# Block products of an MLP: partial sums kept in SBUF, or added to DRAM by DMA

## The chip, the cores and the metric

The kernel runs on one core of a Trainium2 chip. The metric is device time in microseconds (us), the median over runs of the whole kernel. One execution was profiled; its trace gives the start, the duration and the waits of the instructions of each engine: TensorE (PE; its weight loads are PEld), VectorE (DVE), ScalarE (ACT), GpSimd (POOL) and SyncE (SP), which issues DMAs.

## The reference

The input x has 2048 rows of 576 numbers. It is normalized by rows, goes through an MLP with 4608 hidden features and through a two-dimensional Fourier transform of which the real part is kept, and all three are summed:

```python
xn = _layernorm(x, axis=-1)
# A: a = xn @ dft_hid_re.T, b = xn @ dft_hid_im.T
#    y = dft_seq_re @ a - dft_seq_im @ b
# B: relu(xn @ w1) @ w2
return x + A(xn) + B(xn)
```

All arrays are float32.

## The kernel before

Every float32 operand of a matmul is split into a high and a low float16 part, and three products of parts stand for one product. The work has three stages.

The **MLP** runs first. The hidden features are cut into NB = 9 blocks b of 512, the rows into NG = 4 groups g of 512; a step is one (b, g), 36 in all. `mlp1_step` makes the first layer of a step in four parts i, each of 128 hidden features by 512 rows (L292, L317). `mlp1_out` takes them through the ReLU and the splits to SBUF (L332 to L343). `mlp2` makes the second layer. It is a Strassen-Winograd scheme: each operand is cut into 2 x 2 blocks, and the four blocks of the product C (row half `row`, column half `col`, each 256 rows by 288 columns, held as 128 partitions x 2 x 288) come out of seven products n = 0 to 6. `PRODUCTS` says which block of C a product belongs to, and `PLACE` says in which PSUM buffer it is summed:

```python
    PRODUCTS = [
        (A11, B11, True, 0, 0),
        (A12, B21, True, 0, 0),
        (S2, T2, False, 0, 1),
        (S1, T1, True, 1, 1),
        (S3, T3, False, 1, 1),
        (S4, B22, False, 0, 1),
        (A22, T4, False, 1, 0),
    ]
    PLACE = [0, 1, 0, 3, 0, 3, 0]
```

So the first buffer goes on collecting products 0, 2, 4 and 6, and after each product the sum so far is read out and counts towards one block of C: products 0 and 1 to block (0,0), 2 and 5 to (0,1), 3 and 4 to (1,1), 6 alone to (1,0). Two buffers of the pool `ps2` hold the three places in turn. Each read-out is one VectorE instruction (L363) that scales by `us[b]` and adds to the accumulator `accs[g]` in SBUF. `accs[g]` holds four tiles of 128 rows of x (loaded at L80, and the input of the normalization), so x itself is the start value of the sum. After the last block of a group, four DMAs on SP store the tiles to the DRAM tiles `spill` (L366).

Steps are interleaved: the first layer of a step stands between products of the step before (part i, then products 2i and 2i + 1). Beside them run pieces of `todo`, one at a time: loading, scaling and splitting the next block's weights. For these, the largest magnitude is taken (L99, L414), brought across the partitions by GpSimd (L105, for blocks 2 and up; for blocks 0 and 1 by PE, L142 and L150) and read by VectorE (L108; L152, L424). In block 0 the groups 1 to 3 are also normalized on the way (statistics L184 to L206, `normalize` L226 and L227, `remainder` on GpSimd L231 and L234, `transposes` L242 to L252). The matrices of the sequence transform, C, are read once for their magnitude (`first_c`, `sum_c`: tile f, L665 and L672).

The **hidden transform** (`dft1`, L760 to L792) follows, and its results R lie in the SBUF space of the released pools. The **sequence transform** (L857 to L883) multiplies R by the matrices C, again in seven products, onto tiles `o`, which `load_out` fills from `spill` (L853), and stores them.

The order on each engine is made by the tile framework's scheduler when the kernel is built; each engine then works through its own list in that order. `tc.issue_after(order["acc"])` puts some instructions behind the last L363 issued.

Of the kernel before, what the change touches and what calls it, by code (L numbers as in the profile page):

```python
# [1 line left out]

# [7 lines left out]
F32 = mybir.dt.float32  # L10
BF16 = mybir.dt.bfloat16
I32 = mybir.dt.int32
AF = mybir.ActivationFunctionType
ALU = mybir.AluOpType
# [3 lines left out]
P = 128  # L18
S = 2048
D = 576  # L20
DFF = 4608
NT = S // P
FB = 512
NB = DFF // FB
# [3 lines left out]
NG = S // G  # L28
TG = G // P
# [4 lines left out]
EH = D // 2  # L34
# [7 lines left out]
def kernel(  # L42
# [17 lines left out]
    nc = tc.nc  # L60
# [3 lines left out]
    dram = ctx.enter_context(tc.tile_pool(name="dram", bufs=1, space=bass.MemoryType.DRAM))  # L64
# [8 lines left out]

    accs = [accp.tile([P, TG, D], F32, name=f"acc{g}") for g in range(NG)]
    acc = [accs[t // TG][:, t % TG] for t in range(NT)]
    spill = [dram.tile([P, D], F32, name=f"spill{t}") for t in range(NT)]
    raws = {}

    def load_x(t):
# [92 lines left out]
    means, factors, shifts, order = {}, {}, {}, {}  # L172
# [115 lines left out]
    w1s, w2s, us, hs = {}, {}, {}, {}  # L288

    def mlp1_group(b, g, i, cols, ps, wk=WK, start=True, stop=True):  # L290
        for n, (kx, hl, k) in enumerate(wk):
            nc.tensor.matmul(  # L292
                ps[:, cols], w1s[b, i // 2][:, hl, i % 2 * KT + k], xT[g][:, kx, cols],
                start=(start and n == 0), stop=(stop and n == len(wk) - 1),
            )

    def new_ps1(b, g, i):
        return ps1.tile([P, G], F32, tag="ps1", name=f"p1_{b}_{g}_{i}")

    def mlp1(b, g, i):  # L300
        ps = new_ps1(b, g, i)
        mlp1_group(b, g, i, slice(0, G), ps)
        return ps
# [38 lines left out]
        order["s"] = nc.scalar.activation(hi, st[:, 1:], AF.Copy).ins  # L342
        order["lo"] = nc.vector.tensor_tensor(lo, st[:, 1:], hi, ALU.subtract).ins  # L343

    places = {}

    def mlp2(b, g, n):

        qa, qb, first, row, col = PRODUCTS[n]
        if first:  # L350
            places[n] = ps2.tile([P, 2, 512], F32, tag="ps2", name=f"p2_{b}_{g}_{n}")[:, :, :EH]
        ps = places[PLACE[n]]
        for c in range(2):
            for i in range(NQ):
                h, w = hs[b, g, i], w2s[b, i]
                for j, (x, y) in enumerate(((0, 0), (0, 1), (1, 0))):
                    nc.tensor.matmul(  # L357
                        ps[:, c], h[:, x, qa, c * P : (c + 1) * P], w[:, y, qb],
                        start=first and i == 0 and j == 0, stop=i == NQ - 1 and j == 2,
                        skip_group_check=not first,  # L360
                    )
        o = accs[g].rearrange("p (h c) (j e) -> p h j c e", h=2, j=2)[:, row, col]
        order["acc"] = nc.vector.scalar_tensor_tensor(o, ps, us[b], o, ALU.mult, ALU.add).ins  # L363
        if b == NB - 1 and n == 6:
            for t in range(g * TG, (g + 1) * TG):
                nc.sync.dma_start(spill[t], acc[t])  # L366

    sc, pw, mx = {}, {}, {}

# [140 lines left out]
    ps = [ps1.tile([P, G], F32, tag="ps1", name=f"p1_0_0_{i}") for i in range(NF)]  # L510
# [86 lines left out]
    T(10)  # L597
    T(11)
    early = [mlp1(0, 2, 0), mlp1(0, 2, 1)]
    for q in range(7):  # L600
        mlp2(0, 0, q)

# [47 lines left out]
    NP = NT // 2  # L650
# [28 lines left out]
    for n in range(2, len(steps)):  # L679
        b, g = steps[n]  # L680
# [15 lines left out]
        ps = []  # L696
        for i in range(NF):
            if n == 2:
                ps.append(early.pop(0) if early else mlp1(b, g, i))
            else:  # L700
                mlp1_step(b, g, i, ps)
            if i % 2:
                mlp1_out(b, g, i // 2, *ps[i - 1 : i + 1])
            if b == 0 and g + 1 < NG:
                t = (g + 1) * TG + i
                normalize(t)
                remainder(t, nc.gpsimd)
                transposes(t)
            if n == 2 and i == 2:
                todo += prepare_block(1)  # L710
            for _ in range(1 if b else 3):
                work()
            for q in range(2 * i, min(2 * i + 2, 7)):
                mlp2(pb, pg, q)
            for _ in range(1 if b else 3):
                work()
            if n > 3 and i % 2 and passes:
                passes.pop(0)()
    while todo:
        work()  # L720
    for q in range(7):
        mlp2(*steps[-1], q)
# [127 lines left out]
    def load_out(p):  # L850
        o = outs[p] = op.tile([P, 2, D], F32, tag="o", name=f"o{p}")
        for h in range(2):
            nc.sync.dma_start(o[:, h], spill[p + h * NP])  # L853

    AHEAD = 3
    load_out(0)
    for n, (p, kh) in enumerate(units):  # L857
        if kh == 0 and p + 1 < NP:
            load_out(p + 1)
        if n + 1 < len(units):  # L860
            load_c(n + 1)
        for i, (q, rq, first, row, col) in enumerate(PRODUCTS):
            m = n * 7 + i
            if m + AHEAD < 7 * len(units):
                operand(m + AHEAD)
            if first:
                places[i] = bank(f"p{n}_{i}")
            ps, w = places[PLACE[i]], csp[m]
            for k in range(HK):
                r = R[kh * HK + k]  # L870
                for j, (a, c) in enumerate(((0, 0), (0, 1), (1, 0))):
                    nc.tensor.matmul(  # L872
                        ps, w[:, a, k], r[:, c, rq],
                        start=first and k == 0 and j == 0, stop=k == HK - 1 and j == 2,
                        skip_group_check=not first,
                    )
            o = outs[p][:, row, col * EH : (col + 1) * EH]
            nc.vector.scalar_tensor_tensor(o, ps, us["c"][:, n : n + 1], o, ALU.mult, ALU.add)  # L878
            if kh and i in (2, 4, 5, 6):
                h, j = ((0, 0), (1, 1), (0, 1), (1, 0))[(2, 4, 5, 6).index(i)]  # L880
                rows = slice((p + h * NP) * P, (p + h * NP + 1) * P)
                e = slice(j * EH, (j + 1) * EH)
                nc.sync.dma_start(out[rows, e], outs[p][:, h, e])  # L883
# [54 lines left out]
```

## Time and profile before

| | us |
|---|---|
| median of 3 runs | 1285.52 (1283.52 to 1285.96) |
| the profiled execution | 1283.83 |
| its span, first to last instruction | 1282.0 |
| PE, DVE, ACT, POOL busy | 1264.8, 980.5, 539.0, 36.5 |
| a step of the MLP, from block 1 on | 22.16 |
| the sequence transform on PE | 329.3 |

Busy times are unions of the instructions' times; the instructions of a stage overlap between engines, so they do not add up to the span. An engine's idle time matters only where the chain of waits that ends last goes through it. A group's row gives the line, the engine, the operation, output <- input, the shapes, the count, then busy time, mean ns of one, idle time before them and what ended most of it.

### The profile page before, as it was taken

How to read it: one execution, taken by the hardware profiler on the slowest of the kernel's cores; microseconds unless marked ns; L12 is line 12 of the kernel's file. 1: busy time of each engine (PE TensorE's matmuls, PEld its weight loads, DVE VectorE, ACT ScalarE, POOL GpSimd, SP SyncE). 2: the span in 40 equal slices, each digit the busy share in tenths (PEclk: the TensorE clock that was granted, in tenths of full speed). 3: DMA queues.
4: the chain of work that ended last, by engine and by line, in shares of the span. 5: the costliest groups of instructions: out<-in, count | busy, mean ns of one | idle time of the engine just before them, and what ended most of it. 6: DMA issues, size and time to landing. Idle time of an engine off the chain costs nothing.

```text
span 1282.0 us, 21851 instructions
## 1 busy us (share of the span) xinstructions
PE 1264.8 (99%) x9164; PEld 859.2 (67%) x9164; DVE 980.5 (76%) x1671; ACT 539.0 (42%) x794; POOL 36.5 (3%) x60
## 2 busy tenths in 40 slices
PE   8799999999999999999999999999999999999998
PEld 7565665666565665666565665677777777777777
DVE  8978877786686687777867868568678788888875
ACT  5834443343443443434434434244443333333332
POOL 2310000000000000000000000000000000000000
PEclk8999999999999999999999999999999999999999
DMA  6102112221221222122222213330033435334320
GB/s 243 43 1 68 56 59 91 86 77 65 87 91 68 64 79 68 69 91 87 69 73 86 97 57 110 112 132 17 1 114 124 155 101 167 121 125 133 130 85 19
DMA packets 38002, 112.75 MB, mean 88 GB/s; under 512 B 3984, under 2 KB 10640, under 8 KB 37904
## 3 DMA queue, kind: packets, MB, share of 16 engines
q1 hardware_dynamic: 37904, 111.36, 25.9%
q8 instruction: 71, 1.16, 0.4%
q14 instruction: 27, 0.22, 0.0%
HBM read 101.91 MB, written 9.44 MB: 87 GB/s over the span
## 4 chain that ended last, share of the span: by engine, by line
PE 91%; DVE 5%; ACT 1%; DMA 1%; issue 1%; SPq 0%; POOL 0%; POOLq 0%; ACTq 0%; DVEq 0%
PE p L292 29%; PE p L357 27%; PE p L872 26%; PE pd L760 7%; PE p L317 1%; DVE acc L363 1%; DVE w2s L167 1%; DVE xn L226 0%; DVE w1s L167 0%; DMA acc<-in_x_dram 0%; DVE st L184 0%; DMA c<-in_cre_dram 0%; DVE h L336 0%; PE pd L770 0%; ACT xn L227 0%
## 5 line engine op out<-in xcount | busy, mean ns | idle before, releaser
L292 PE MATMUL p<-xT,w1s 128*128 128x512 f16 (+1 forms) x2136 | 434.7, 355 | 1.3 <-ACT xT L249 1.1
L357 PE MATMUL p<-w2s,h 128*128 128x288 f16 x3024 | 394.6, 286 | 2.0 <-ACT xT L252 1.0
L357 PEld LDWEIGHTS <-h 128*128 128x128 f16 x3024 | 295.3, 98 | 103.0 <-issue 2.8
L872 PE MATMUL p<-R,cs 128*128 128x288 f16 x2688 | 329.4, 286 | 0.0
L292 PEld LDWEIGHTS <-w1s 128*128 128x128 f16 x2136 | 193.5, 98 | 201.9 <-issue 18.4
L872 PEld LDWEIGHTS <-cs 128*128 128x128 f16 x2688 | 263.0, 98 | 66.3
L363 DVE SCALAR_TENSOR_TENSOR acc<-p,c_ub,acc 128x576 f32<-128x576 f32 x252 | 204.8, 813 | 39.0 <-PE p L357 38.5
L166 ACT ACTIVATE cs<-c,sc_c 128x1024 f16<-128x1024 f32 x112 | 128.5, 1148 | 200.2 <-PE p L872 147.5
L167 DVE SCALAR_TENSOR_TENSOR cs<-c,sc_c,cs 128x1024 f16<-128x1024 f32 x112 | 143.7, 1283 | 50.3 <-ACT cs L166 50.1
L336 DVE SCALAR_TENSOR_TENSOR h<-p,h 128x256 f16<-128x256 f32 (+1 forms) x144 | 79.8, 555 | 94.8 <-ACT h L335 94.5
L342 ACT ACTIVATE h<-s 128x1024 f16<-128x1024 f32 x72 | 76.1, 1057 | 160.5 <-DVE s L340 160.4
L335 ACT ACTIVATE h<-p 128x256 f16<-128x256 f32 (+1 forms) x144 | 69.9, 486 | 147.2 <-PE p L292 141.4
L343 DVE TENSOR_TENSOR h<-s,h 128x1024 f16<-128x1024 f32 x72 | 88.1, 1224 | 31.2 <-ACT h L342 30.2
L760 PE MATMUL pd<-dsp,xT 128*128 128x288 f16 x832 | 104.0, 286 | 0.2
L760 PEld LDWEIGHTS <-xT 128*128 128x128 f16 x832 | 80.7, 98 | 22.6 <-issue 2.5
L878 DVE SCALAR_TENSOR_TENSOR o<-p,us_c,o 128x288 f32<-128x288 f32 x112 | 57.6, 514 | 20.3 <-PE p L872 20.3
L672 ACT ACTIVATE f<-f 128x1024 f32<-128x1024 f32 x64 | 66.6, 1041 | 3.7 <-DMA f<-in_cre_dram 3.7
L332 ACT ACTIVATE s<-p 128x256 f32<-128x256 f32 x72 | 27.4, 380 | 74.0 <-PE p L317 54.5
L166 ACT ACTIVATE w2s<-raw_w,c_sw 128x576 f16<-128x576 f32 (+1 forms) x54 | 44.2, 851 | 25.9 <-DVE raw_w L445 15.4
L167 DVE SCALAR_TENSOR_TENSOR w2s<-raw_w,c_sw,w2s 128x576 f16<-128x576 f32 (+1 forms) x54 | 48.5, 916 | 7.6 <-ACT w2s L166 7.6
L167 DVE SCALAR_TENSOR_TENSOR w1s<-raw_w,c_sw,w1s 128x640 f16<-128x640 f32 x36 | 30.8, 892 | 9.8 <-ACT w1s L166 9.8
L166 ACT ACTIVATE w1s<-raw_w,c_sw 128x640 f16<-128x640 f32 x36 | 27.9, 817 | 24.0 <-DVE c_sw L109 23.6
(106 smaller groups left out, 672.5 us busy)
## 6 DMA issues: line engine op xcount, KB each, us to landing
f<-in_cre_dram SPq DMA_DIRECT2D x32, 512.0 KB, 3.5
f<-in_cim_dram SPq DMA_DIRECT2D x32, 512.0 KB, 3.5
c<-in_cre_dram SPq DMA_DIRECT2D x32, 512.0 KB, 4.0
c<-in_cim_dram SPq DMA_DIRECT2D x32, 512.0 KB, 4.6
raw_w<-in_w_dram SPq DMA_DIRECT2D x17, 640.0 KB, 4.0
raw_w<-in_w_dram SPq DMA_DIRECT2D x18, 576.0 KB, 3.8
acc<-in_x_dram SPq DMA_DIRECT2D x16, 288.0 KB, 7.4
spill<-acc SPq DMA_DIRECT2D x16, 288.0 KB, 2.5
```

The source lines that it names most:

```text
L166: nc.scalar.activation(hi, src, AF.Copy, scale=s)
L167: nc.vector.scalar_tensor_tensor(lo, src, s, hi, ALU.mult, ALU.subtract)
L292: nc.tensor.matmul(ps[:, cols], w1s[b, i // 2][:, hl, i % 2 * KT + k], xT[g][:, kx, cols], start=(start and n == 0), stop=(stop and n == l ...
L335: nc.scalar.activation(hi, src, AF.Relu)
L336: stt(lo, src, 0.0, hi, ALU.max, ALU.subtract)
L342: order["s"] = nc.scalar.activation(hi, st[:, 1:], AF.Copy).ins
L343: order["lo"] = nc.vector.tensor_tensor(lo, st[:, 1:], hi, ALU.subtract).ins
L357: nc.tensor.matmul(ps[:, c], h[:, x, qa, c * P : (c + 1) * P], w[:, y, qb], start=first and i == 0 and j == 0, stop=i == NQ - 1 and j == 2 ...
L363: order["acc"] = nc.vector.scalar_tensor_tensor(o, ps, us[b], o, ALU.mult, ALU.add).ins
L672: nc.scalar.activation(f, f, AF.Abs, scale=2.0**-10, accum_out=sums_c[:, n, q : q + 1])
L760: nc.tensor.matmul(ps[j], xT[g][:, kx, c * P : (c + 1) * P], dsp[j][:, hl, k], start=(t % 2 == 0 and n == 0), stop=(t % 2 == 1 and n == le ...
L872: nc.tensor.matmul(ps, w[:, a, k], r[:, c, rq], start=first and k == 0 and j == 0, stop=k == HK - 1 and j == 2, skip_group_check=not first,)
```

## The change

The accumulator over blocks moves from SBUF to DRAM. For each group and each block of C there is now one DRAM tile of `spill`, and x is copied into it from DRAM by 16 DMAs on SP before the first product is read out (`spill_x`). In each step, the first product of a block of C (n = 0, 2, 3, 6) is scaled by ScalarE into one of four slots of `accs[0]`, which are taken in turn; the second (n = 1, 5, 4) is scaled and added there by VectorE; then one DMA on GpSimd's queue adds the slot to the DRAM tile. Product 6 has no second. The stores behind the last block go away, and `load_out` reads half rows from two tiles.

```diff
-    spill = [dram.tile([P, D], F32, name=f"spill{t}") for t in range(NT)]
+    spill = {
+        (g, row, col): dram.tile([P, TG // 2, EH], F32, name=f"spill{g}_{row}{col}")
+        for g in range(NG) for row in range(2) for col in range(2)
+    }
...
-    places = {}
+    places, sums = {}, {}
+    turns = itertools.count()
+
+    def spill_x(g):
+        for row in range(2):
+            for col in range(2):
+                src = x[(g * TG + row * 2) * P : (g * TG + row * 2 + 2) * P, col * EH : (col + 1) * EH]
+                nc.sync.dma_start(spill[g, row, col], src.rearrange("(c p) e -> p c e", p=P))
...
-        o = accs[g].rearrange("p (h c) (j e) -> p h j c e", h=2, j=2)[:, row, col]
-        order["acc"] = nc.vector.scalar_tensor_tensor(o, ps, us[b], o, ALU.mult, ALU.add).ins
-        if b == NB - 1 and n == 6:
-            for t in range(g * TG, (g + 1) * TG):
-                nc.sync.dma_start(spill[t], acc[t])
+        if n in (0, 2, 3, 6):
+
+            sums[row, col] = accs[0][:, next(turns) % TG].rearrange("p (c e) -> p c e", e=EH)
+            nc.scalar.activation(sums[row, col], ps, AF.Copy, scale=us[b])
+        else:
+            o = sums[row, col]
+            order["acc"] = nc.vector.scalar_tensor_tensor(o, ps, us[b], o, ALU.mult, ALU.add).ins
+        if n not in (0, 2, 3):
+            nc.gpsimd.dma_start(spill[g, row, col], sums[row, col], accum_op=ALU.add)
...
     early = [mlp1(0, 2, 0), mlp1(0, 2, 1)]
+    for g in range(NG):
+        spill_x(g)
     for q in range(7):
         mlp2(0, 0, q)
...
-            nc.sync.dma_start(o[:, h], spill[p + h * NP])
+            g, c = divmod(p + h * NP, TG)
+            for col in range(2):
+                nc.sync.dma_start(o[:, h, col * EH : (col + 1) * EH], spill[g, c // 2, col][:, c % 2])
```

## The prediction

> **What bounds the kernel now.** I read the page's head first, then busy time by stretch, then who waits for whom on TensorE, then the timeline of the stretches where TensorE is not full.
>
> ```profile
> span 1282.0 us, 21851 instructions
> ...
> PE 1264.8 (99%) x9164; PEld 859.2 (67%) x9164; DVE 980.5 (76%) x1671; ACT 539.0 (42%) x794; POOL 36.5 (3%) x60
> ...
> L363 DVE SCALAR_TENSOR_TENSOR acc<-p,c_ub,acc 128x576 f32<-128x576 f32 x252 | 204.8, 813 | 39.0 <-PE p L357 38.5
> ```
>
> TensorE (PE) is busy 1264.8 of 1282.0 us, so 17.2 us is all that any relief of the other engines could return, whatever it takes off them. L363 is the instruction that the change splits up.
>
> ```profile
> 0.00:30.00 30.00, 25.65 (x313) 22.84 (x314) 26.97 (x100) 16.41 (x27) 6.19 (x12) 0.89 0.71 259
> 30.00:60.00 30.00, 22.97 (x303) 18.37 (x301) 27.50 (x62) 27.03 (x47) 12.48 (x16) 1.00 0.10 27
> 60.00:90.00 30.00, 29.23 (x215) 19.93 (x213) 24.34 (x51) 10.46 (x18) 6.00 (x8) 1.00 0.05 20
> 90.00:124.50 34.50, 33.09 (x207) 18.02 (x206) 27.16 (x60) 17.64 (x28) 0.00 (x0) 1.00 0.13 39
> 434.50:456.66 22.16, 22.16 (x141) 13.35 (x140) 17.30 (x37) 11.71 (x20) 0.37 (x1) 1.00 0.15 48
> 812.00:845.00 33.00, 32.80 (x237) 22.56 (x236) 19.45 (x34) 8.13 (x16) 0.40 (x1) 1.00 0.32 115
> 845.00:949.50 104.50, 104.31 (x869) 80.36 (x867) 76.20 (x128) 49.69 (x80) 0.00 (x0) 1.00 0.08 29
> 949.50:1279.00 329.50, 329.25 (x2688) 262.75 (x2686) 262.38 (x288) 126.80 (x113) 0.00 (x0) 1.00 0.37 123
> ```
>
> Columns: stretch, its length, busy time (and count) of PE, PEld, DVE, ACT, POOL, then granted clock, DMA share and GB/s. The idle time of PE is 4.35 + 7.03 us before 60 us, ahead of the first product that the change touches; 0.77 + 1.41 us up to 124.5; nothing in the steady steps (one step, 22.16 us, is full to the last hundredth); 0.20 us in 812 to 845, 0.19 us and 0.25 us behind it, and 3.0 us of last stores. The change can reach 0.77 + 1.41 + 0.20 + 0.19 + 0.25 = 2.8 us.
>
> ```profile
> 73.56 3.10 PE L357 MATMUL p<-w2s,h 128*128 128x288 f16 x24 [0.64 <-DVE acc L363]
> 76.50 0.67 PE L242 MATMUL pt<-ident,xn 128*128 128x128 f16 x9
> ...
> 86.86 3.10 PE L357 MATMUL p<-w2s,h 128*128 128x288 f16 x24
> ...
> 111.76 0.27 PE L142 MATMUL pm<-ident,mb 128*1 128x128 bf16 x2 [1.03 <-DVE mb L424]
> ```
>
> These are the only waits over half a microsecond after 60 us: one for L363 itself, in block 0, and one for the scales of the next block's weights.
>
> **What goes and comes, per step (36 steps, numbered by block b and row group g).** Seven L363 at 0.81 us leave three; DVE loses 4 x 0.81 = 3.25 us, in all 144 x 0.813 = 117 us. ScalarE (ACT) gains four scaled copies of 128x576 from PSUM. No such row exists. L335 takes 0.38 us for 256 columns and 0.60 for 512, that is 0.86 ns a column and 0.66 us for 576; L780, which takes its scale from a tile as the new line does, has 0.50 us for 288, so 0.50 + 288 x 0.86 ns = 0.75 us. I take 0.75, the nearer form: 4 x 0.75 = 3.0 us a step, 108 us in all. In the step shown DVE goes from 17.3 to 14.1 and ACT from 11.7 to 14.7 of 22.16 us. Neither becomes the bound, and the DVE time was not on the path: a full PE returns nothing. Effect: 0.
>
> **PSUM release in a steady step.** PE's next write to a bank now waits for ACT where it waited for DVE. In the step shown, products 0 and 1 run at 434.5, 2 and 3 at 440.91, 4 and 5 at 446.66, 6 at 452.40, the next 0 at 456.68. Between two products on one bank lie 12 matmuls of 0.12 us and, in most cases, the 13 of the first layer (2.8 us), so a copy has 1.4 to 4.2 us. In the order of the changed kernel the copy of product 0 stands behind L672 (1.04 + 0.19 us), which in a heavy step ended at 459.96; then 0.75 us, and product 2 starts at 462.5. About 1.8 us are left. Behind a waiting copy stand L342 and the next L332/L335, whose results are needed some 5 us later. Effect: 0, and if that cover is gone, one microsecond of delay would be a microsecond a step.
>
> **The adding DMAs.** 144 of 288 KB go to POOL's queue. The trace has neither an adding DMA nor one issued from POOL. For its landing, L, the low end is a plain store of this size, 2.5 us, and the middle is store plus load, since it reads its target first: 2.5 + 3.2 = 5.7. The high end is twice that, 11.4. I take 5.7. For POOL's work per DMA, g, the low end is SP's issue of the four stores, 2.07 / 4 = 0.5 us, the high end twice POOL's longest usual row (L234, 1.16 us), 2.3; I take 1.2, one such row. In a steady step a buffer returns after one turn of four: product 2's is released by product 5's add at 451.15 and must be rewritten, 0.75 us included, before product 4 of the next step at 446.66 + 22.16 = 468.82, so POOL and DMA have 16.9 us against 1.2 + 5.7 = 6.9. Partition maxima (L105) now queue on POOL with the DMAs; in two of three places in a block they stand a whole DMA issue later than the sum before them, and DVE, which waits in L108, has the 8 us of the step that it is idle. Bandwidth: queue 1 moved 111.36 MB in 25.9% of 1282 us, 2.98 us a MB, 0.88 us for 0.295 MB; at three moves each, four DMAs take 10.6 of 22.16 us beside the 0.15 to 0.23 share that is there. The loads of f land after 3.5 us and are used 10.7 us after issue; they may double. Effect: 0.
>
> **Block 0, the one tight place.** Its first steps follow each other faster: products 2 and 3 of group 1 come 13 us after those of group 0, and POOL still has the four remainders L231/L234 of group 3 (1.5 us each, 70.6 to 76.6). The changed order puts the first adding DMA ahead of them and the next three behind. Step by step: product 1's add moves to about 69.6 (the root L194 now stands behind a 0.75 us copy), POOL issues until 70.8, ACT's interleaved copies deliver the last normalized tile at 74.5, the last remainder ends near 77.6; then the DMAs of products 4 and 5 are issued, and the buffer of product 5 is free at 77.6 + 2 x 1.2 + 5.7 = 85.7. Product 2 of group 1 must be copied into it before product 4 at 87.03: start by 86.3. It fits, by 0.6 us. The transposes at 76.50 and later have their tiles by 73. Meanwhile product 5 of group 0, now behind ACT's copy at 73.05 instead of the DVE add, starts 0.5 us earlier than 73.56: -0.5. At 111.76 the matmul that waits for L424 stands two matmuls of each layer earlier in PE's order, so it waits some 2 x 0.213 + 2 x 0.12 = 0.7 us longer, the load that it hangs on being as late as before: +0.7.
>
> [...] The four normalizations L226 (median 0.57 us for 576 columns, against 0.81 of L363 for as many) run at 69.8 to 72.5, beside the first DMA issue from POOL. If POOL cannot work on an issue while they run, it ends up to 4 x 0.57 = 2.3 us later, and all that is queued behind it; that is the second rival below. [...]
>
> **The rest.** The 16 copies from x to DRAM follow the x loads on SP (from 18.6 us); the DMA share is 0.10 in 30 to 60 us, and the next load behind them that anyone awaits is issued at 56.2: 16 x 288 KB, read and written, is 9.4 MB x 2.98 = 28 us. Effect 0. The 16 stores leave SP, four of which stood ahead of the loads of C at 841.74 for 2.07 us; 16 more loads of half size come, 8 us or more ahead of use. The first R tile (L788, 851.77) now lies where the last DMAs read: last copy near 842.3, plus 1.2 and 5.7 is 849.2, and its bank is wanted at 862. Effect 0.
>
> Sum: -0.5 + 0.7 = +0.2. The profiled execution took 1283.83 us (span 1282.0 and 1.83 around it), and the median shown is 1.69 above that; the sum goes on the median: 1285.52 + 0.2 = 1285.7. A measurement here tells 0.2%, 2.6 us, from no change.
>
> **Rivals.**
> - *Block 0's buffers come back late; slower.* It decides where 2g + L passes 86.3 - 77.6 = 8.7 us; mine is 8.1, and both terms are unseen. Against it: a plain store lands in 2.5. Each us above is a PE us, once. At the high ends, 2 x 2.3 + 11.4 = 16.0: +7.3, 1293.0. Chance 0.22.
> - *POOL is held by L226.* Buffer free at 88.0 instead of 85.7: 1.7 us late, 1287.4. Chance 0.08.
> - *The DMAs bound the step; slower.* Above 5.5 us of all 16 engines each, four do not fit into 22.16 us; at 7 us a step takes 28, +5.84 x 34 = +199, 1484. Against: 2.6 us estimated. Chance 0.06.
> - *PE's small gaps close; faster.* All 2.8 us reachable: 1282.7. For: 0.64 us waits for L363. Against: the 1.03 us hangs on a load. Chance 0.08.
> - *The change does not do what it says:* its order shows 144 copies, 108 adds, 144 DMAs. 0.01.
> - A wait in ACT's queue or a DMA's that I do not see, slower by some us: 0.09.
>
> My forecast, no change, has the remaining 0.46.
>
> **Numbers.** Range 1282.9 to 1294.0: it takes in the first two rivals and most of the fourth, and leaves out the third and the tails. Faster 0.08. Slower 0.22 + 0.06 + 0.09 + 0.01 from the second rival's upper part = 0.38. Same 0.54.
>
> **What would show it.** PE idle only before 124.5 us and steps still 22.16 us; copies near 0.75 us on ACT; adding DMAs landing in 3 to 8 us. Wrong: idle of PE ended by ACT copies that wait for a DMA, near 87 us or in every step; a step longer than 22.2 us; waits for L108 that reach PE.

## The result and the profile after

The changed kernel takes 1292.38 us (1290.38 to 1293.37) against 1285.13 us (1283.52 to 1285.96) of the kernel before, the ratio 1.0056 with a 95% interval of 1.0039 to 1.0073. It is slower by 0.56%. The profiled execution has a span of 1290.2 us against 1282.0, 8.2 us more.

The page of the changed kernel, head and costliest groups:

```profile
span 1290.2 us, 22323 instructions
...
PE 1266.0 (98%) x9164; PEld 859.6 (67%) x9164; DVE 882.0 (68%) x1527; ACT 635.2 (49%) x938; POOL 159.3 (12%) x204
...
L385 POOL DMA_DIRECT2D spill<-acc x144 | 126.1, 893 | 623.6 <-DVE acc L383 481.0
...
L380 ACT ACTIVATE acc<-p,c_ub 128x576 f32<-128x576 f32 x144 | 104.4, 735 | 74.2 <-PE p L372 72.2
L383 DVE SCALAR_TENSOR_TENSOR acc<-p,c_ub,acc 128x576 f32<-128x576 f32 x108 | 87.4, 816 | 73.1 <-PE p L372 65.7
```

VectorE lost 98 us of busy time and ScalarE gained 96, as intended, and neither is near full. PE's busy time barely moved, so the 8 us are times in which PE stood, or ran at a lower clock. Busy time by stretch of the changed kernel (columns as before; the last stretches are those of the last step, the hidden transform and the sequence transform):

```profile
60.00:90.00 30.00, 29.92 (x219) 20.36 (x217) 19.15 (x46) 15.38 (x25) 11.27 (x14) 1.00 0.41 71
90.00:124.50 34.50, 32.37 (x210) 18.39 (x208) 24.34 (x56) 20.61 (x32) 4.63 (x6) 1.00 0.43 78
434.50:456.66 22.16, 22.16 (x142) 13.32 (x141) 17.21 (x38) 13.57 (x23) 3.83 (x5) 1.00 0.54 99
812.00:844.00 32.00, 30.20 (x214) 20.33 (x212) 13.22 (x26) 12.70 (x21) 5.98 (x8) 1.00 0.54 103
844.00:955.00 111.00, 108.44 (x888) 82.97 (x887) 76.49 (x128) 50.37 (x80) 1.37 (x2) 0.98 0.13 33
955.00:1287.00 332.00, 330.07 (x2694) 263.28 (x2691) 262.36 (x288) 126.92 (x113) 0.00 (x0) 1.00 0.38 122
```

The steady step is still 22.16 us and full, with a DMA share of 0.54 where it was 0.15. (VectorE's 17.21 us there, against 17.30, do not show what it saved: other pieces of the next block's preparation fall into this step now. The totals above show it.) PE starts on the last step's products at 829.17 us; in the kernel before it did so at 829.06. Up to there the change costs 0.1 us in this execution; runs below with the same order up to this point came to it at 829.02 to 830.16 us, so a difference as small as 0.1 is partly chance. All else is lost behind it. The timeline of PE there, with what ended each stop:

```profile
840.79 3.31 PE L372 MATMUL p<-w2s,h 128*128 128x288 f16 x24 [1.60 <-ACT acc L380]
...
857.59 0.28 PE L781 MATMUL pd<-dsp,xT 128*128 128x288 f16 x1 [0.66 <-DVE R L810]
858.44 0.28 PE L781 MATMUL pd<-dsp,xT 128*128 128x288 f16 x1 [0.57 <-DVE R L810]
860.06 6.12 PE L781 MATMUL pd<-dsp,xT 128*128 128x288 f16 x35 [1.34 <-DVE R L810]
...
971.77 3.47 PE L895 MATMUL p<-R,cs 128*128 128x288 f16 x27 [1.44 <-DVE o L901]
```

ScalarE's timeline over the first two places shows what stood ahead of the awaited instructions (the bracket is ScalarE's own idle time ahead of the row):

```profile
838.97 1.06 ACT L693 ACTIVATE f<-f 128x1024 f32<-128x1024 f32 x1 [1.94 <-DMA f<-in_cre_dram]
839.93 0.19 ACT L693 ACTIVATION_READ_ACCUMULATOR f<-f 128x1 f32 x1
840.02 0.72 ACT L380 ACTIVATE acc<-p,c_ub 128x576 f32<-128x576 f32 x1
...
855.45 1.15 ACT L171 ACTIVATE cs<-c,sc_c 128x1024 f16<-128x1024 f32 x1 [2.26 <-DMA c<-in_cim_dram]
856.51 0.87 ACT L809 ACTIVATE R<-pd,c_rho 128x288 f16<-128x288 f32 x2
```

First place: product 3's copy (840.02) is behind the magnitude sum of the last tile f, which waited for its load. Second: the first R copies (L809), which empty the PSUM banks that PE wants at 857, are behind the second split of C (L171), which waited for a load of C. (L171 splits a float32 tile of C into float16 parts; L693 sums magnitudes for its scale.) Those loads land late. The DMAs from 836 to 862 us (size and median us from issue to landing), before:

```profile
spill<-acc SPq DMA_DIRECT2D x4, 288.0 KB, 2.5
c<-in_cre_dram SPq DMA_DIRECT2D x2, 512.0 KB, 5.8
c<-in_cim_dram SPq DMA_DIRECT2D x2, 512.0 KB, 5.9
```

and after:

```profile
spill<-acc POOLq DMA_DIRECT2D x4, 288.0 KB, 6.4
c<-in_cre_dram SPq DMA_DIRECT2D x2, 512.0 KB, 9.2
c<-in_cim_dram SPq DMA_DIRECT2D x2, 512.0 KB, 10.0
```

Behind the stop at 857 to 860 the granted clock (the column behind POOL's) is low, in stretches of 1 us:

```profile
861.00:862.00 1.00, 1.00 (x7) 0.62 (x6) 1.00 (x2) 0.00 (x0) 0.00 (x0) 0.53 0.06 16
862.00:863.00 1.00, 1.00 (x6) 0.64 (x5) 0.97 (x2) 0.00 (x0) 0.00 (x0) 0.50 0.00 0
863.00:864.00 1.00, 1.00 (x6) 0.64 (x5) 1.00 (x2) 0.30 (x1) 0.00 (x0) 0.50 0.00 0
864.00:865.00 1.00, 1.00 (x8) 0.72 (x7) 1.00 (x4) 1.00 (x2) 0.00 (x0) 0.77 0.00 0
```

That is 0.47 + 0.50 + 0.50 + 0.23 = 1.7 us lost although PE was busy. The account: 0.1 up to 829; 1.6 in the last step; 0.66 + 0.57 + 1.34 = 2.6 in the hidden transform; 1.7 by the clock; 1.4 at 970, where a VectorE addition on C (L842) waited 3.11 us for its load ahead of the read-out L901; 0.4 behind the last matmul. Of 8.2 us these are 7.8.

To compare runs whose times up to the last step differ by chance, I use the tail below: from the first product of the last step (829.17 us here) to the end of the last matmul. It is 449.7 us in the kernel before and 457.3 in the changed one.

### The profile page after: what moved, and what is told of

It reads as the page before. It is cut to its first block, busy times and chain, and to the rows that moved or that the text cites. A ratio compares the mean times of both kernels' runs of the same rounds, so it can differ in the third digit from the quotient of the medians.

```text
span 1290.2 us, 22323 instructions
## 1 busy us (share of the span) xinstructions
PE 1266.0 (98%) x9164; PEld 859.6 (67%) x9164; DVE 882.0 (68%) x1527; ACT 635.2 (49%) x938; POOL 159.3 (12%) x204
## 5 line engine op out<-in xcount | busy, mean ns | idle before, releaser
L171 ACT ACTIVATE cs<-c,sc_c 128x1024 f16<-128x1024 f32 x112 | 128.5, 1148 | 205.1 <-PE p L895 151.0
L385 POOL DMA_DIRECT2D spill<-acc x144 | 126.1, 893 | 623.6 <-DVE acc L383 481.0
L380 ACT ACTIVATE acc<-p,c_ub 128x576 f32<-128x576 f32 x144 | 104.4, 735 | 74.2 <-PE p L372 72.2
L383 DVE SCALAR_TENSOR_TENSOR acc<-p,c_ub,acc 128x576 f32<-128x576 f32 x108 | 87.4, 816 | 73.1 <-PE p L372 65.7
L901 DVE SCALAR_TENSOR_TENSOR o<-p,us_c,o 128x288 f32<-128x288 f32 x112 | 57.5, 514 | 20.3 <-PE p L895 20.3
L693 ACT ACTIVATE f<-f 128x1024 f32<-128x1024 f32 x64 | 66.7, 1042 | 1.9 <-DMA f<-in_cre_dram 1.9
L171 ACT ACTIVATE w2s<-raw_w,c_sw 128x576 f16<-128x576 f32 (+1 forms) x54 | 45.0, 850 | 32.2 <-DVE c_sw L455 15.2
L171 ACT ACTIVATE w1s<-raw_w,c_sw 128x640 f16<-128x640 f32 x36 | 28.7, 821 | 45.7 <-DVE c_sw L114 45.6
```

Source lines behind the costliest of these rows:

```text
L171: nc.scalar.activation(hi, src, AF.Copy, scale=s)
L380: nc.scalar.activation(sums[row, col], ps, AF.Copy, scale=us[b])
L385: nc.gpsimd.dma_start(spill[g, row, col], sums[row, col], accum_op=ALU.add)
```

## Experiments

Theory: nothing runs slower throughout; the adding DMAs delay two loads at the hand-over, and instructions that PE waits for stand in the queues of ScalarE and VectorE behind instructions that wait for these loads. Rivals: the new order on ScalarE by itself; the ScalarE copies by their time; something that runs through the whole kernel.

**The last four adding DMAs left out.**

```diff
-        if n not in (0, 2, 3):
+        if n not in (0, 2, 3) and (b, g) != (NB - 1, NG - 1):
```

> The changed kernel without the four adding DMAs of the last step (8,3); that step's sums never reach DRAM. Every engine's order is otherwise the changed kernel's. Theory (transfer): at the hand-over to the hidden transform the loads of C lie beside the last adding DMAs and land after 9.2 to 10.0 us, where before they landed after 5.8; the second split of C (L171, 855.45) waits for them with the first R copies behind it, and TensorE stops for 2.6 us at 857 to 860, then runs 1.7 us slower in all at a granted clock of about 0.5. Without the four DMAs the loads land after 6 to 6.5 us, the stops at 857 to 860 and the low clock are gone, and the time is 4.3 us shorter, 1288.1. Rival (order): the split's place ahead of the R copies is enough by itself; the order is the same here, so the stops stay and the time is 1292. The waits at 839 (1.60) and 970 (1.44) stay under both.

1287.25 us, ratio to before 1.0028 (1.0016 to 1.0040); the tail is 451.8 us, 5.5 less. No stop is left from 844 to 955 and the clock is 1.00 throughout, in the same order on ScalarE:

```profile
851.27 1.15 ACT L171 ACTIVATE cs<-c,sc_c 128x1024 f16<-128x1024 f32 x1 [0.23 <-DMA c<-in_cim_dram]
852.33 0.87 ACT L809 ACTIVATE R<-pd,c_rho 128x288 f16<-128x288 f32 x2
```

The loads of C landed after 5.0 and 5.1 us. So the transfers make the wait, and the new order alone costs nothing at this place. The stop in the last step stayed (1.78 us); the one at 970 shrank to 0.43, which I had not expected.

**Splits of C behind the R copies.** `order["R", m]` is the last copy (L812) of R tile m.

```diff
-        split(w[:, 0], w[:, 1], src, sc["c"][:, n : n + 1])
+        with tc.issue_after(order["R", m]) if m < 4 else nullcontext():
+            split(w[:, 0], w[:, 1], src, sc["c"][:, n : n + 1])
```

> The changed kernel with the first four splits of C (L171) put behind the last copy (L812) of R tiles 0 to 3 in ScalarE's queue; all transfers as in the changed kernel. Theory (transfer and queue together): C still lands after 9 to 10 us, but nothing that TensorE needs stands behind it; first R copies at about 853 (when the last adding DMA has read the space of the first R tile) in place of 856.5, stops at 857 to 860 under 0.4 us, no low clock, 1288.1. Rival (shared space): it is the first R tile's space, which the last adding DMAs still read, that holds the copies; then the first R copy stays at 856 or later and the stops stay, 1292.

1288.95 us, ratio 1.0039 (1.0025 to 1.0053); tail 455.3. ScalarE and PE:

```profile
856.62 0.89 ACT L809 ACTIVATE R<-pd,c_rho 128x288 f16<-128x288 f32 x2 [3.79 <-DMA spill<-acc]
```

```profile
841.59 4.77 PE L372 MATMUL p<-w2s,h 128*128 128x288 f16 x24 [2.45 <-ACT acc L380]
...
860.13 6.16 PE L781 MATMUL pd<-dsp,xT 128*128 128x288 f16 x49 [0.69 <-DVE R L810]
```

The stop fell from 2.6 to 0.69 + 0.18 us and no low clock follows it. The first R copy comes at the same time, 856.62 against 856.51. But the whole stage began 2.3 us later here (846.20 against 843.94), so within its stage the copy comes 2.2 us earlier. It now waits for the last adding DMA, whose source lies where the first R tile is put. Both theory and rival hold a part. The loads of C landed after 7.4 and 7.7 us here, not the 9 to 10 expected, so part of the gain can be theirs. The last step's stop happened to be 2.45 us here, and a low clock followed that one: its 24 matmuls took 4.77 us against 3.31.

**The last magnitude sum behind product 3's copy.**

```diff
-            nc.scalar.activation(sums[row, col], ps, AF.Copy, scale=us[b])
+            ins = nc.scalar.activation(sums[row, col], ps, AF.Copy, scale=us[b]).ins
+            if (b, g, n) == (NB - 1, NG - 1, 3):
+                order["s"] = ins
```

> The changed kernel with the last magnitude sum of C (L693) put behind the copy of product 3 of the last step in ScalarE's queue. Theory: in the changed kernel this copy stood behind the sum, which waited 1.94 us for its load (838.97); the 1.60 us of TensorE before the last two products vanish, the copy comes at about 837.8, everything behind is 1.6 us earlier and otherwise unchanged (stops at 857 to 860 less 1.6 in time, same 2.6 us long): span 1288.6. Rival: the wait moves to the next late one (product 4's add or the scales of C), span 1290.

Span 1287.7 us in a single execution, tail 455.0. The copy came at 837.61 and the 1.60 us are gone. The stops at 855 to 859 became 1.44 + 0.57 + 1.34 us, since C landed as late as before (9.4 and 10.2 us) and PE came to it earlier; the low clock behind them stayed.

**Loads of C ahead of the next o tiles.**

```diff
-        if kh == 0 and p + 1 < NP:
-            load_out(p + 1)
         if n + 1 < len(units):
             load_c(n + 1)
+        if kh == 0 and p + 1 < NP:
+            load_out(p + 1)
```

> The changed kernel with the loads of the next unit of C issued ahead of the next pair of o tiles. Theory: the 1.44 us of TensorE at 970 come from the eight half-size o loads (4.24 us of issue on SP) ahead of the loads of C; with only the first four o loads ahead the loads of C are issued about 2.1 us earlier and that wait is gone: span 1288.8. Rival: the bytes in flight decide, not the place in SP's queue; then 1 us or more of the wait stays, span 1290.

Span 1289.7 us in a single execution, tail 455.9, 1.5 us less: PE did not stop at 970. That the edit did this is not shown. With the changed kernel's order on SP the stop there was 1.44 us once and 1.30, 1.23, 0.53, 0.43, 0.29, 0.24, 0.16 and 0 us in eight other runs of this study, so it comes and goes without the edit; and with the edit and others, PE still stopped 0.54 us at 966 (the run of four edits together, below). The span hides part of the gain, because the first 124 us took 1 us longer here.

**The slots moved away from the first R tiles, with the splits behind the R copies.**

```diff
-            sums[row, col] = accs[0][:, next(turns) % TG].rearrange("p (c e) -> p c e", e=EH)
+            sums[row, col] = accs[NG - 1 if b else 0][:, next(turns) % TG].rearrange("p (c e) -> p c e", e=EH)
...
+    ra0 = tc.alloc_tile_pool(name="ra0", bufs=1)
     rpool = [tc.alloc_tile_pool(name="ra", bufs=1)]
...
-        R[t] = rpool[-1].tile([P, 2, 7, EH], F16, name=f"R{t}")
+        R[t] = (ra0 if t < 3 else rpool[-1]).tile([P, 2, 7, EH], F16, name=f"R{t}")
```

(`accs` also gets a pool for each tile, so that its parts are tracked apart.)

> The splits of C behind the R copies, as in the run with that edit alone, where the first R copy still waited 3.79 us for an adding DMA (856.62) and TensorE stopped for 0.87 us; and the slots of the sums moved to accs[3] from block 1 on, so that the first three R tiles share no space with them. Theory (the rest of the stop is the shared space): the first R copy comes at about 854, no stop over 0.2 us between 850 and 870. Rival (the banks come free late by the chain of R copies itself): the stop of 0.7 us stays. The wait at 839 stays under both, 1.6 to 2.5 us.

Span 1289.0 us in a single execution, tail 455.6. The first R copy came at 852.01, so the shared space was a real wait; yet PE stopped 1.89 us, which neither side had. One wait had stood behind the other: an addition on C (`operand`) on VectorE waited 4.12 us for its load, with the last read-out of R tile 0 behind it.

**These edits together.** The diff is the last four.

> The changed kernel with four edits together: splits of C behind the R copies, the last magnitude sum behind the copy of product 3, loads of C ahead of the next o tiles, and from block 1 on the slots of the sums in accs[3], so that the first three R tiles do not lie in space that the last adding DMAs still read. Theory (the loss is four places at the hand-overs, and a low clock behind a stop of over 2 us): all stops from 826 us on are under 0.3 us, no low clock; as long as the kernel before, ratio 0.999 to 1.001. Rival (something runs through the whole kernel, the adding DMAs beside everything): ratio 1.003 or more with steady steps over 22.16 us or small stops in the sequence transform.

1285.47 us against 1284.74, ratio 1.0009 (1.0000 to 1.0018). The steps are 22.16 us and the clock 1.00, so nothing runs through the kernel. The theory's "under 0.3 us" was missed: in the profiled execution, the longest of eleven, PE still stopped 1.67 us at 856 and 0.54 us at 966. VectorE at the first:

```profile
854.97 1.23 DVE L846 TENSOR_TENSOR c<-c,c 128x1024 f32<-128x1024 f32 x1 [3.89 <-DMA c<-in_cre_dram]
856.11 0.51 DVE L814 SCALAR_TENSOR_TENSOR R<-pd,c_rho,R 128x288 f16<-128x288 f32 x1
```

**VectorE's queue too.** All of `operand` is put behind: for the first four pieces behind the last copy and the last low half (`"Rl"`) of an R tile, then behind the read-out (`"o"`) of the product four before.

```diff
+    def operand(m):
+        if m < 4:
+            with tc.issue_after(order["R", m]), tc.issue_after(order["Rl", m]):
+                operand_now(m)
+        else:
+            with tc.issue_after(order["o", m - 4]):
+                operand_now(m)
```

> The run with four edits, and one more: in VectorE's queue too, the pieces that prepare C (the additions and the low halves, `operand`) stand behind the R tile of their turn, and in the sequence transform behind the read-out of the product four before. In the run with four edits TensorE still stopped 1.67 us at 856 and 0.54 us at 966, each time because a VectorE addition on C waited for its load (3.89 and 2.96 us) ahead of read-outs of PSUM. Theory (late C harms only through what stands behind it in a queue): C still lands after 9 to 10 us, yet no stop over 0.3 us is left from 826 us to the end; ratio 0.998 to 1.0005. Rival (C is needed by TensorE itself at that time, or the strict order starves the sequence transform): stops over 0.5 us, waiting for cs; ratio over 1.001.

1284.34 us against 1283.78, ratio 1.0005 (0.9996 to 1.0014). C landed after 8.2 and 9.1 us, late as ever, and PE's windows are full:

```profile
844.00:857.00 13.00, 13.00 (x110) 10.04 (x109) 6.41 (x12) 4.72 (x9) 1.47 (x2) 1.00 0.80 221
857.00:870.00 13.00, 13.00 (x111) 10.05 (x109) 11.16 (x18) 7.03 (x11) 0.00 (x0) 1.00 0.01 1
870.00:955.00 85.00, 85.00 (x710) 65.90 (x708) 61.72 (x108) 41.04 (x66) 0.00 (x0) 1.00 0.04 11
955.00:980.00 25.00, 25.00 (x206) 19.97 (x205) 20.71 (x23) 8.97 (x8) 0.00 (x0) 1.00 0.52 186
```

The tail is 449.1 us (before: 449.7). So the loss was what stood behind the late loads, and the space that the adding DMAs shared with the first R tiles; how much each of the two holds is not separated. The kernel before was not run with these orders, so what they would give it is open. The 98 us taken off VectorE bring nothing, also when nothing else is in the way: PE was already full.

**The first read-outs on VectorE, adding DMAs kept.**

```diff
-            nc.scalar.activation(sums[row, col], ps, AF.Copy, scale=us[b])
+            nc.vector.tensor_scalar(sums[row, col], ps, us[b], None, ALU.mult)
```

> The changed kernel with the first read-out of each block of C scaled by VectorE (tensor_scalar) in place of ScalarE; adding DMAs as before. ScalarE's order then has both first splits of C ahead of the first copy c12 of the hidden transform. Theory: the 1.60 us at 839 vanish, since no read-out stands behind the magnitude sum; but the second split still waits for C until about 854 (C lands after 9 to 10 us beside the last adding DMAs), and now all of R tile 0's chain is behind it: 4 to 5 us of stops at 857 to 862 instead of 2.6, and the low clock behind them: 1291 to 1294. Rival (the ScalarE half costs the time, by its 108 us): back to 1285.

1293.06 us, ratio 1.0070 (1.0057 to 1.0084). The last step's stop is 0.20 us, as before the change; in the hidden transform PE stopped for 4.1 us and the clock was 0.50 behind it:

```profile
859.59 0.28 PE L781 MATMUL pd<-dsp,xT 128*128 128x288 f16 x1 [2.35 <-DVE R L810]
860.44 0.40 PE L781 MATMUL pd<-dsp,xT 128*128 128x288 f16 x1 [0.57 <-DVE R L810]
862.00 8.39 PE L781 MATMUL pd<-dsp,xT 128*128 128x288 f16 x49 [1.16 <-DVE R L810]
```

PE also stopped in block 0, where it had not in the changed kernel:

```profile
76.06 3.10 PE L372 MATMUL p<-w2s,h 128*128 128x288 f16 x24 [2.46 <-DVE acc L380]
```

That read-out stood on VectorE behind two normalizations (L231) which took 3.4 us. PE came to the last step's products at 831.32 us, 2.2 us later than in the changed kernel, so about that much of this run's loss lies ahead of the hand-over; the tail is 456.8. With ScalarE's copies gone the tail is about as long as with them (457.3), so their time is not the cause. That the adding DMAs are is what the runs without them show, above and below; here the order on ScalarE was another too.

**Plain stores in place of adding ones.**

```diff
-            nc.gpsimd.dma_start(spill[g, row, col], sums[row, col], accum_op=ALU.add)
+            nc.gpsimd.dma_start(spill[g, row, col], sums[row, col])
```

> The changed kernel with plain stores in place of the 144 adding DMAs, so that each overwrites the sum of the blocks before; issued from the same queue at the same places. Theory (the price of the adding itself: its target is read and written): landing 2.5 to 3.5 us against 4.6, DMA share of a step 0.4 against 0.62; C lands after 6.5 to 7.5 us, the stops at 857 to 860 are under 0.6 us, no low clock: 1288. Rival (any transfer of this size there costs the same): landing 4.5 us, C after 9 us, stops as in the changed kernel, 1292.

1287.13 us, ratio 1.0021 (1.0011 to 1.0030); tail 452.9. They landed after 2.4 us and C after 6.8. The software queue's line (packets, MB, share of 16 engines), here and in the changed kernel:

```profile
q0 software_dynamic: 11520, 42.48, 8.6%
```

```profile
q0 software_dynamic: 20736, 42.48, 24.0%
```

For the same bytes, 8.6% of 1285.8 us over 144 is 0.77 us of all 16 engines for a store, and 24.0% of 1290.2 is 2.15 us for an adding one. The last step's stop fell to 0.27 us, those in the hidden transform to 0.8 us in all. The rest is mainly the stop at 967, 1.30 us here.

**Every adding DMA issued twice.**

```diff
-            nc.gpsimd.dma_start(spill[g, row, col], sums[row, col], accum_op=ALU.add)
+            for _ in range(2):
+                nc.gpsimd.dma_start(spill[g, row, col], sums[row, col], accum_op=ALU.add)
```

> The changed kernel with every adding DMA issued twice, so that each sum goes into DRAM twice. One adding DMA takes 24.0% of 1290 us over 144, 2.15 us of all 16 engines. Theory (the step is not bound by DMAs, with little left): 8 x 2.15 = 17.2 us, and the 0.15 to 0.23 share of the kernel before (3.3 to 5.1 us), 20.5 to 22.3 us in a step of 22.16: steps stay at 22.2 to 22.6 us, stops grow at block 0 and at the hand-overs, 1300 to 1315. Rival (the slots come back late: each pair of DMAs on one queue lands one behind the other): steps of 23 us or more, with ScalarE's copies waiting for DMAs, 1320 or more.

1492.23 us: as the rival said, but far beyond its 1320. The waits:

```profile
POOL spill L386 <- DMA spill<-acc: 620.3, 142, 8.5
```

The second of a pair goes to the same DRAM tile, so POOL waits for the landing of the first, 4.4 us in the mean, and everything on its queue with it. The wait is set by the program, which has the second of a pair wait for the first. A step takes some 5.9 us more ((1490.5 - 1290.2) / 34), a part of it by a low clock: PE now stopped in the middle of the work of steps, and the clock fell behind such stops:

```profile
485.81 4.37 PE L372 MATMUL p<-w2s,h 128*128 128x288 f16 x24 [2.87 <-ACT acc L380]
```

```profile
486.00:487.00 1.00, 1.00 (x6) 0.62 (x5) 0.27 (x1) 1.00 (x2) 0.36 (x1) 0.50 0.00 0
```

The DMA share was 0.71 to 0.81, so this run doubled a wait in the queue rather than load the engines to their bound, and it doesn't tell how much room they have.

**Stops made on purpose in full work.**

```diff
-            nc.scalar.activation(sums[row, col], ps, AF.Copy, scale=us[b])
+            for _ in range({(4, 1): 5, (5, 1): 7, (6, 1): 9}.get((b, g), 1) if n == 0 else 1):
+                nc.scalar.activation(sums[row, col], ps, AF.Copy, scale=us[b])
```

> The changed kernel with ScalarE's copy of product 0 made 5 times in step (4,1), 7 times in (5,1) and 9 times in (6,1), so that TensorE has to wait for a bank in the middle of full work: 4, 6 and 8 extra copies of 0.74 us are 3.0, 4.4 and 5.9 us against the 1.4 to 4.2 us that a copy has; stops of 0 to 1.2, 0.2 to 2.6 and 1.7 to 4.1 us. Theory (a stop of over about 2 us by itself lowers the granted clock): behind a stop up to 1.8 us the clock stays 1.00; behind one of 2.4 us or more it is 0.5 for 3 to 4 us, which costs 1.5 to 2 us more. Rival (the low clock belongs to the hand-over, where the work changes): 1.00 behind all three.

> The run with three stops again, with 8 copies of product 0 in step (4,1), 9 in (5,1) and 13 in (6,1). The first try left only stops of 0.65 us (7 copies) and 0.69 us (9 copies), at clock 1.00; each further copy adds up to 0.74 us: about 2 us in (4,1) and (5,1), 3.6 us in (6,1). At the hand-over, single stops of 1.60 to 1.99 us left the clock at 1.00, and stops of 2.45 us or 2.5 to 4.1 us in three pieces brought it to about 0.5 for 3 to 4 us. Theory (a long stop by itself lowers the granted clock): 1.00 behind the two of about 2 us, 0.5 for 3 to 4 us behind the one of 3.6. Rival (it takes the hand-over): 1.00 behind all three.

Neither made a long stop in mid-work. With up to 13 copies the stops were 0.65 to 0.99 us, since the scheduler put matmuls of the next first layer ahead; the clock stayed 1.00. The run above with its doubled DMAs did make them: behind 2.87 us at 485.81 the clock was 0.50, and 24 matmuls took 4.37 us instead of 3.10. So the rival is refuted: a low clock does not need the hand-over.

In the second of the two runs the last step gave a single stop of 2.00 us, and a low clock behind it:

```profile
846.03 4.77 PE L372 MATMUL p<-w2s,h 128*128 128x288 f16 x24 [2.00 <-ACT acc L381]
```

Yet the 2.46 us at 76.06 in the run with the read-outs on VectorE left it at 1.00. The length of the stop does not decide. The low phases do not begin at a stop's end: in the changed kernel's trace they begin at 17.96, 35.03 and 861.05 us, the last of them 0.99 us after PE had started again, and these times lie 5 and 242 times 3.413 us apart. Cut along such a grid of 3.41 us, the stop of 2.00 us lies in one window with all of its length:

```profile
842.67:846.08 3.41, 1.41 (x13) 1.00 (x11) 0.22 (x1) 1.78 (x3) 0.31 (x1) 1.00 0.54 96
846.08:849.49 3.41, 3.41 (x15) 2.17 (x15) 1.78 (x6) 0.00 (x0) 0.97 (x2) 0.50 0.14 8
```

The stop of 2.46 us is spread over two windows, 1.08 and 1.38 us:

```profile
71.27:74.68 3.41, 2.33 (x19) 1.67 (x18) 3.41 (x2) 2.17 (x3) 3.19 (x5) 1.00 0.64 87
74.68:78.09 3.41, 2.03 (x17) 1.64 (x17) 2.51 (x5) 0.00 (x0) 3.13 (x5) 1.00 0.00 0
```

## Why the prediction was wrong, and where it was right

- **Steady steps, right.** 22.16 us and full; a copy takes 0.74 us (0.75 predicted).
- **The adding DMAs, right in effect.** POOL spends 0.86 us (1.2 predicted), they land after 4.6 us in the median (5.7), and each takes 2.15 us of all engines (2.6). The step has room for them.
- **Block 0, right.** The tight slot came back at 84.70 us (85.7 predicted, needed by 86.3); the copy waited 0.61 us for it and PE not at all. The wait for L363 is gone (0.64; I had counted 0.5), the one at 111.78 is 1.63 us against 1.03 (+0.6; predicted +0.7). Up to 829 us the sum is +0.1 against +0.2, closer than the terms deserve: in seven other runs with this order the wait at 111.78 was 0.96 to 1.55 us.
- **POOL and the normalizations.** The first adding DMA took 1.51 us beside four L231 (70.06 to 72.11), the usual one 0.86; the rival's 2.3 us did not come. That POOL cannot work on an issue beside them, the condition of that rival, is shown by no run: the one DMA beside them took 0.65 us longer, but it was also the first of its queue, and the longest of all, 1.74 us, came at 78.33 with no normalization beside it.
- **PSUM release, wrong in the last step.** "About 1.8 us are left" behind the magnitude sum held only while that sum does not itself wait. The last load of f, issued at 833.97, ended ScalarE's wait only at 838.97. (In the kernel before ScalarE waited 3.67 us for such a load too, but no read-out stood behind it.) I had written of these loads that "they may double", but against steady steps alone, and had not asked who stands behind the sum: +1.6.
- **"The rest", wrong.** "Effect 0" for the loads of C and the first R tile is the step that failed. I had priced the adding DMAs' bandwidth for a steady step alone, gave the loads of C beside the last of them no price, and looked only at the R tile's space. The loads of C, issued at 844.18 beside the last three adding DMAs, landed after 9.2 to 10.0 us, not 5.8, and in the changed order a split of C stands ahead of the three first L809. That was to be read from the order on ScalarE. The first R tile was not safe either: without C in the way it waits until 856.62. Cost: 2.6 us of stops, and 1.7 us of a lower clock, for which the sum had no term.
- **The o loads.** In time themselves, but eight issues in front of the loads of C (4.24 us of SP against 2.59). The stop at 970, 1.4 us here and anything from 0 to 1.3 in other runs, hung here on a late load of C; whether the o issues made them late stays open.

The named rivals did not happen: block 0 is in time and the DMAs do not bound the step. What came is the last, unnamed one, a wait in ScalarE's queue or a DMA's, to which I gave 0.09; the sign that I had named for it, idle of PE ended by ScalarE copies that wait for a DMA, was there, but at 839 and 857 us and not at 87 or in every step. The forecast was no change, and the time lies 7 us above it, well outside the 2.6 us that I had called the noise. That the range holds it is luck: its high end was the price of late buffers in block 0, which did not happen.

## What to carry to other kernels

A load that has spare time in the kernel before can lose it when a change adds DMA traffic beside it (the loads of C landed after 9.2 to 10.0 us here, and after 5.8 to 5.9 before), and the price is not its lateness but what stands behind its first user in that engine's queue. So read each stage's hand-over in the changed order, engine by engine, and ask of every instruction that waits for a DMA which PSUM read-outs are queued behind it. And relief of an engine that does not bound, here 98 us of VectorE, can at best give back PE's idle time.

## What the runs showed of the hardware

- **The clock after a stop.** In the traces of the kernel before and of the changed one, the clock of 0.50 came in phases of 3.41 us or of twice that: from 16.33 to 23.16 us before, and for 3.41 us each from 17.96, 35.03 and 861.05 us after, these three on one grid of 3.41 us. What went with it is how much of one window of the grid PE stood idle, in one piece or several. In these two traces the windows at full clock with 1.88, 1.91, 2.21 and 2.41 us of idle were each followed by one at 0.50, those with 1.83 us or less never. So the bound lies a little above half a window here, an estimate from these numbers. Single stops of 2.00 us (the second run with stops made on purpose) and 2.45 us (the splits behind the R copies) lowered the clock, and one of 2.46 us, spread over two windows (the read-outs on VectorE), did not. A low phase cost 1.5 to 1.7 us beside the stop (24 matmuls took 4.77 us instead of 3.31; the sum of 1.7 above).
- **Adding costs.** An adding DMA of 288 KB took 2.8 times the engine time of a plain store (2.15 against 0.77 us of 16 engines) and landed after 4.4 to 4.6 us against 2.4. A load of 512 KB beside the last adding ones landed after 7.4 to 10.4 us over the runs, after 6.8 beside plain stores and after 5.0 to 5.1 with neither.
- **Two adds to one target.** Where the program had the second wait for the first, POOL's queue stood meanwhile, 4.4 us in the mean. What two adds do without that wait was not run.
